# Other transfer costs in a planner, one column of weights ahead of the values, and VectorE subtracting the maximum of two tiles

## The chip, the cores and the metric

The kernel runs on one core of a Trainium2 chip. TensorE (PE) multiplies matrices, VectorE (DVE), ScalarE (ACT) and GpSimd (POOL) work on elements, and SyncE (SP) issues the transfers between the chip's memory (HBM) and the on-chip buffer (SBUF); TensorE writes its results to PSUM, which VectorE and ScalarE read. Each engine runs its instructions in the order in which they are written, and waits at an instruction until all that it needs is there. The metric is the device time of one execution in microseconds (us).

## The reference

Attention over 2 batches of 8 heads, 768 tokens, 64 numbers a head; each token sees the tokens less than 16 away, and 24 summaries, one for each block of 32 tokens (the maximum of the keys, the mean of the values). Two layers of a multilayer network follow, over 1536 tokens of 512 numbers with 2048 inner ones:

```python
k_sum = k.reshape(B, H, nb, block, D).max(axis=3)
v_sum = v.reshape(B, H, nb, block, D).mean(axis=3)
scores_l = scale * np.matmul(q, k.transpose(0, 1, 3, 2))       # masked to |i - j| < 16
scores_s = scale * np.einsum('bhsd,bhnd->bhsn', q, k_sum) + np.log(block)
a = softmax(concatenate([scores_l_m, scores_s]))
attn = a @ concatenate([v, v_sum])
...
h = x @ w_in;  g = np.maximum(h, 0.0) + np.log1p(np.exp(-np.abs(h)));  y = g @ w_out
h = np.maximum(y @ w_in2, 0.0);  out = h * h @ w_out2
```

## The kernel before, in words

**Attention.** The 1536 tokens are 12 tiles of 128. For a tile, TensorE multiplies transposed queries `qT` with `kaug` (24 key summaries and a window of 96 keys for each half of the tile, copied from the transposed keys `kT`) into the PSUM tile `sc` (tile 1 into `accp`). The softmax gives `s`, which TensorE transposes into `at`, and `at` times `vwin` (the window of values, and the 24 block means of values in its first partitions) gives the tile's output, kept as a high part `xh` and a residual `xl`. The block means are one product of TensorE from the whole values of a batch (`late`), copied to `vsum` and from there into `vwin`.

**Two ways through the softmax.** The letter of `STYLE` says which one a tile takes. In `m` (tiles 0 and 1) TensorE adds the mask itself, VectorE takes the negated maximum of a half tile (`mx`), and ScalarE takes the exponential of each of the 4 heads of a half with that maximum as its bias, 16 instructions for two tiles; VectorE then sums (`sm`) and takes reciprocals, and GpSimd multiplies. In `p` (tiles 2 to 11) VectorE adds the mask, GpSimd or VectorE subtracts the maximum, and one exponential does the whole tile.

**The network.** Its first layer's first four columns of weights (step `A`, lines 664 and 701: `h` and `accp`) run between the attention tiles, over 256 tokens at a time; all else runs after the attention, over 512 tokens. All weights and operands are split into a high and a low part and each product is three. A column of weights comes by two transfers of 512 KB into `raw`; its parts are made by `three` (ScalarE or VectorE), two joins on VectorE (line 614), a scaling, a high part (`wih`, `woh`) and a residual (`wil`, `wol`, GpSimd or VectorE).

**The order of the work.** `Plan` is a list scheduler that runs when the kernel is built. Each `op` has engines with an assumed duration, a due time, its inputs and outputs, and for a transfer its size `kb`. `run` moves a modelled time forward; on each engine it takes the ready operation with the earliest due time, chooses between two engines the one that would be done first (VectorE with 1.5 us to its disadvantage), and writes the instructions out in that order. A transfer is modelled as one queue: ready 1.6 us after its issue, `kb`/245 us long, usable 0.3 us later. Where TensorE would idle for more than 0.9 us in the model, `warm` writes filler products on `ident` (line 857). What is written is a fixed order, with the waits that the data need; the modelled times are not in it. `EARLY` is the number of weight columns whose transfers are due ahead of the first batch's values.

Of the kernel before, what the change touches and what calls it, by code (L numbers as in the profile page):

```python
# [13 lines left out]
ALU = mybir.AluOpType  # L14
# [17 lines left out]
KLAG = 6.0  # L32
EARLY = 2
LD_K = (8.0, 0.0)
# [4 lines left out]
DL = 32.0  # L39
PEB = 40.0  # L40
NS_T = 2
STYLE = "mmpppppppppp"

# [10 lines left out]
class Plan:  # L54
# [38 lines left out]
    def run(self, warm, banks, pool):  # L93
# [41 lines left out]
        while any(cand.values()):  # L135
# [27 lines left out]
            if kb:  # L163
                dma = max(dma, end + 1.6) + kb / 245.0
                end = dma + 0.3
            done[i] = end
# [19 lines left out]
def kernel(  # L186
# [192 lines left out]
    def ld_pair(src, u, place, due):  # L379
        b, i = divmod(u, NU)  # L380
        for z in range(2):
            op("SP", 0.6, due, lambda z=z: nc.sync.dma_start(  # L382
                out=PZ(place)[:, z].rearrange("p a (r d) -> p a r d", r=2),
                in_=src[b, 4 * z:4 * z + 4, 256 * i:256 * i + 256, :].rearrange("h (p r) d -> p h r d", r=2)),
                w=[(place, z)], kb=180)

# [42 lines left out]
    def ld_vb(b, due):  # L429
        op("SP", 0.8, due, lambda: nc.sync.dma_start(  # L430
            out=PL["V"], in_=v[b].rearrange("h (p r) d -> p h r d", r=VR)), w=["V"], kb=1017)

# [15 lines left out]
    def vsum_put(x, due):  # L448
        op("POOL", 1.3, due, lambda: nc.gpsimd.tensor_scalar(
            out=vwin[x][0:NS].rearrange("p j h d -> p j (h d)"),  # L450
            in0=vsum.rearrange("p (o x) -> p o x", o=1).to_broadcast([NS, 2, H * D]),
            scalar1=1.0, scalar2=1.0, op0=ALU.mult, op1=ALU.mult), r=["vsum", "z"], w=[("vsw", x)])

    def mk_kaug(t, due):
        i = t % NTB
        for j in range(2):
            c0 = 128 * i + 64 * j
            us = sorted({min(max((c0 + d - 16) // 128, 0), NTB - 1) for d in (0, 95)})
            op("POOL", 0.55, due, lambda j=j, c0=c0: nc.gpsimd.tensor_scalar(
                out=kaug[t % 2][:, :, j, NS:], in0=kT[:, :, c0:c0 + WIN],  # L460
                scalar1=1.0, scalar2=1.0, op0=ALU.mult, op1=ALU.mult),
                r=["z"] + [("kT", u, z) for u in us for z in range(2)], w=[("kw", t % 2, j)])

    def tile_sc(t, due):
# [4 lines left out]
        style = STYLE[t]  # L469
        pe_mask = style in "mn"  # L470

# [32 lines left out]
        for h0, h1 in halves:  # L504
# [14 lines left out]
            if pe_mask:  # L519
# [3 lines left out]
                def exps(hh=hh, sv=sv, mv=mv, rv=rv):  # L523
                    for p in range(NP):
                        nc.scalar.activation(out=sv[:, p], in_=scv(hh)[:, p], func=AF.Exp, bias=mv[:, p:p + 1],
                                             **({"accum_out": rv[:, p:p + 1]} if style == "n" else {}))
                op("ACT", NP * (0.55 if style == "n" else 0.37), due, exps, r=[(sck, hh), *mk],
                   w=sk + (rk if style == "n" else []), tab="exp")
            else:
# [362 lines left out]
```

## Time and profile before

| what | value |
|---|---|
| time, median of 3 (lowest to highest) | 620.82 us (620.57 to 621.85) |
| the profiled execution: its time, its span | 620.8 us, 619.0 us |
| busy in the span: TensorE, VectorE, ScalarE, GpSimd | 602.5, 312.1, 288.2, 202.0 us |
| TensorE's mean granted clock | 0.991 of full |
| chain that ended last, share of TensorE | 84% |
| moved by transfers | 51.34 MB |

Busy time is a sum over the whole span, and only TensorE is near it. The stages differ: attention and step A end near 110 us. In a timeline a row has its start, its duration and, in brackets, the idle time of its engine before it and what ended that. In tables of groups stand the count, the busy time and mean ns of one, and the idle time. L12 is line 12 of the kernel.

### The profile page before, as it was taken

How to read it: one execution, taken by the hardware profiler on the slowest of the kernel's cores; microseconds unless marked ns; L12 is line 12 of the kernel's file. 1: busy time of each engine (PE TensorE's matmuls, PEld its weight loads, DVE VectorE, ACT ScalarE, POOL GpSimd, SP SyncE). 2: the span in 40 equal slices, each digit the busy share in tenths (PEclk: the TensorE clock that was granted, in tenths of full speed). 3: DMA queues.
4: the chain of work that ended last, by engine and by line, in shares of the span. 5: the costliest groups of instructions: out<-in, count | busy, mean ns of one | idle time of the engine just before them, and what ended most of it. 6: DMA issues, size and time to landing. Idle time of an engine off the chain costs nothing.

```text
span 619.0 us, 9449 instructions
## 1 busy us (share of the span) xinstructions
PE 602.5 (97%) x3809; PEld 507.5 (82%) x3809; DVE 312.1 (50%) x449; ACT 288.2 (47%) x501; POOL 202.0 (33%) x197
## 2 busy tenths in 40 slices
PE   9798999999999999999999999999999999999996
PEld 7687988999788888888888888888888888888885
DVE  5788999726664133542146652247542533232332
ACT  4686888856653124542247643346412432221220
POOL 5877696535550042331138440116000410000000
PEclk9798999999999999999999999999999999999999
DMA  9999632423541014340024330114100100010011
GB/s 283 243 281 217 162 74 55 116 69 116 166 128 35 0 35 136 103 136 1 0 64 122 120 103 0 35 61 131 47 1 0 69 0 2 0 58 11 20 50 68
DMA packets 64524, 51.34 MB, mean 83 GB/s; under 512 B 36320, under 2 KB 58848, under 8 KB 64480
## 3 DMA queue, kind: packets, MB, share of 16 engines
q1 hardware_dynamic: 64480, 50.73, 28.6%
q8 instruction: 30, 0.49, 0.3%
q14 instruction: 14, 0.11, 0.1%
HBM read 47.58 MB, written 3.15 MB: 82 GB/s over the span
## 4 chain that ended last, share of the span: by engine, by line
PE 84%; DVE 8%; DMA 4%; ACT 2%; SPq 1%; issue 1%; POOL 0%; DVEq 0%; POOLq 0%
PE h L664 40%; PE accp L701 21%; PE acc L701 18%; DMA late<-in_v_dram 2%; DMA vwin<-in_v_dram 2%; DVE raw L614 2%; DVE mx L530 1%; DVE s L499 1%; PE ab L439 1%; PE ab L561 1%; DVE sm L516 1%; SPq L382 1%; PE ab L547 1%; DVE xl L571 0%; DVE sm L517 0%
## 5 line engine op out<-in xcount | busy, mean ns | idle before, releaser
L664 PE MATMUL h<-xh,wih 128*128 128x512 f32 (+1 forms) x432 | 159.9, 370 | 0.0
L664 PE MATMUL h<-xh,wil 128*128 128x512 f32 (+1 forms) x432 | 158.7, 367 | 0.0
L664 PE MATMUL h<-xl,wih 128*128 128x512 f32 (+1 forms) x432 | 158.7, 367 | 0.0
L614 DVE SCALAR_TENSOR_TENSOR raw<-raw 128x512 uint32<-128x512 uint32 x128 | 113.3, 902 | 52.8 <-ACT raw L609 39.8
L664 PEld LDWEIGHTS h<-xh,wih 128*128 128x128 f32 x432 | 81.5, 189 | 14.6 <-issue 0.6
L664 PEld LDWEIGHTS h<-xh,wil 128*128 128x128 f32 x432 | 81.3, 188 | 13.9
L664 PEld LDWEIGHTS h<-xl,wih 128*128 128x128 f32 x432 | 81.4, 188 | 13.7
L673 ACT ACTIVATE e<-h 128x512 f32<-128x512 f32 x48 | 28.8, 599 | 125.4 <-PE h L664 125.4
L675 DVE SCALAR_TENSOR_TENSOR h<-h,e 128x512 f32<-128x512 f32 x48 | 33.5, 698 | 103.2 <-ACT e L673 103.1
L671 ACT ACTIVATE h<-h 128x512 f32<-128x512 f32 (+1 forms) x60 | 29.8, 499 | 83.2 <-PE h L664 83.1
L308 POOL TENSOR_SCALAR wih<-raw 128x512 fp32r<-128x512 f32 x18 | 12.6, 703 | 150.5 <-PE h L664 142.1
L623 POOL TENSOR_TENSOR wol<-raw,woh 128x512 fp32r<-128x512 f32 x30 | 42.6, 1421 | 48.9 <-ACT woh L306 48.3
L623 POOL TENSOR_TENSOR wil<-raw,wih 128x512 fp32r<-128x512 f32 x31 | 42.6, 1374 | 28.9 <-ACT wih L306 27.4
L609 ACT ACTIVATE raw<-raw 128x512 uint32<-128x512 uint16 x59 | 39.3, 670 | 13.2 <-DMA raw<-in_moe_w_out_dram 7.5
L680 DVE TENSOR_TENSOR g1l<-h,g1h 128x512 fp32r<-128x512 f32 (+1 forms) x40 | 24.2, 606 | 31.9 <-ACT g1h L678 31.8
L723 DVE TENSOR_TENSOR part<-accp,part 128x512 f32<-128x512 f32 x24 | 16.0, 686 | 43.5 <-PE accp L701 43.5
L680 DVE TENSOR_TENSOR g2l<-h,g2h 128x512 fp32r<-128x512 f32 x28 | 19.3, 690 | 33.7 <-ACT g2h L678 33.5
L306 ACT ACTIVATE raw<-raw 128x512 f32<-128x512 f32 x41 | 27.5, 673 | 18.7 <-DVE raw L614 18.7
L680 DVE TENSOR_TENSOR g0l<-h,g0h 128x512 fp32r<-128x512 f32 (+1 forms) x40 | 24.1, 605 | 21.1 <-ACT g0h L678 20.9
L678 ACT ACTIVATE g0h<-h 128x512 fp32r<-128x512 f32 (+1 forms) x40 | 21.2, 534 | 16.4 <-DVE h L675 16.0
L536 POOL TENSOR_TENSOR s<-s,sm 128x960 f32<-128x960 f32 (+1 forms) x14 | 22.1, 1580 | 13.9 <-DVE sm L518 13.0
L678 ACT ACTIVATE g1h<-h 128x512 fp32r<-128x512 f32 (+1 forms) x40 | 21.4, 534 | 9.2 <-DVE h L675 8.9
(172 smaller groups left out, 1175.4 us busy)
## 6 DMA issues: line engine op xcount, KB each, us to landing
raw<-in_moe_w_in_dram SPq DMA_DIRECT2D x32, 512.0 KB, 4.2
raw<-in_moe_w_out_dram SPq DMA_DIRECT2D x32, 512.0 KB, 3.4
vwin<-in_v_dram SPq DMA_DIRECT2D x20, 192.0 KB, 5.7
part<-in_k_dram SPq DMA_DIRECT2D x12, 256.0 KB, 4.9
late<-in_v_dram SPq DMA_DIRECT2D x2, 1536.0 KB, 11.3
out_dram<-part SPq DMA_DIRECT2D x12, 256.0 KB, 2.1
part<-in_q_dram SPq DMA_DIRECT2D x10, 256.0 KB, 5.1
vwin<-in_v_dram SPq DMA_DIRECT2D x4, 160.0 KB, 5.2
```

Of the source, the lines that this page charges most:

```text
L306: nc.scalar.activation(out=out_, in_=in_, func=AF.Copy, **({} if mul is None else {"scale": mul}))
L536: op(("POOL", "DVE"), (1.8 * n + 0.1, 1.75 * n), due, lambda e, sv=sv, rv=rv, spread=spread: tt(e).tensor_tensor(out=sv, in0=sv, in1=sprea ...
L609: nc.scalar.activation(out=lo, in_=q4[:, :, 1], func=AF.Copy, scale=2.0 ** -13, bias=-4095.5 / 8192.0)
L614: nc.vector.scalar_tensor_tensor(out=lo, in0=hi, scalar=n, in1=lo, op0=how, op1=ALU.bitwise_or)
L623: op(("POOL", "DVE"), (1.4, 1.0), dv, lambda e: tt(e).tensor_tensor(out=ws[s][kl], in0=lo.bitcast(F32), in1=ws[s][kh].bitcast(F32), op=ALU ...
L664: nc.tensor.matmul(out=hview(st), lhsT=ws[s][wn][:, w_], rhs=xx[bl][:, kk, o:o + n], start=(kk == 0 and xx is xh and wn == "ih"), stop=(kk ...
L671: op("ACT", ta, due, lambda: nc.scalar.activation(out=hview(st), in_=hview(st), func=AF.Softplus), w=[H_], tab="sp")
L673: op("ACT", ta, due, lambda: nc.scalar.activation(out=e_t[st["g"] % 2], in_=hview(st), func=AF.Relu), r=[H_], w=[("e", st["g"] % 2)])
L675: op("DVE", tv, due, lambda: nc.vector.scalar_tensor_tensor(out=hview(st), in0=hview(st), scalar=0.0, in1=e_t[st["g"] % 2], op0=ALU.max, o ...
L678: op("ACT", ta, due, lambda: nc.scalar.activation(out=gview(st)[0], in_=hview(st), func=AF.Copy), r=[H_] + need, w=gk[0])
L680: op("DVE", tv, due, lambda: nc.vector.tensor_tensor(out=gview(st)[1], in0=hview(st), in1=gview(st)[0].bitcast(F32), op=ALU.subtract), r=[ ...
L701: nc.tensor.matmul(out=o, lhsT=a[:, sl], rhs=b, start=(st["first"] and c == 0 and not (A and m % 2)), stop=(st["last"] and c == 2 and not ...
```

## The change

The planner's transfer model is changed: a transfer is ready 1.2 us after its issue and usable 1.5 us after its end (1.6 and 0.3 before), and the sizes that stand for paired keys and queries and for the whole values are larger. One column of weights instead of two is due ahead of the values. The window copies `kaug` may go to VectorE as well, and the copies of block means `vsum_put` to ScalarE. Tiles 0 and 1 take the new way `d`: the mask is still added by TensorE, VectorE adds the negated maximum from PSUM into `s`, and one exponential does a half tile.

```diff
-EARLY = 2
+EARLY = 1
+KAUG_E = ("POOL", "DVE")
-STYLE = "mmpppppppppp"
+STYLE = "ddpppppppppp"
...
-                dma = max(dma, end + 1.6) + kb / 245.0
-                end = dma + 0.3
+                dma = max(dma, end + 1.2) + kb / 245.0
+                end = dma + 1.5
...   (ld_pair)
-                w=[(place, z)], kb=180)
+                w=[(place, z)], kb=206)
...   (ld_vb)
-            out=PL["V"], in_=v[b].rearrange("h (p r) d -> p h r d", r=VR)), w=["V"], kb=1017)
+            out=PL["V"], in_=v[b].rearrange("h (p r) d -> p h r d", r=VR)), w=["V"], kb=1090)
...
-        op("POOL", 1.3, due, lambda: nc.gpsimd.tensor_scalar(
-            out=vwin[x][0:NS].rearrange("p j h d -> p j (h d)"),
-            in0=vsum.rearrange("p (o x) -> p o x", o=1).to_broadcast([NS, 2, H * D]),
-            scalar1=1.0, scalar2=1.0, op0=ALU.mult, op1=ALU.mult), r=["vsum", "z"], w=[("vsw", x)])
+        op(("POOL", "ACT"), (1.15, 1.0), due, lambda e: copy(
+            e, vwin[x][0:NS].rearrange("p j h d -> p j (h d)"),
+            vsum.rearrange("p (o x) -> p o x", o=1).to_broadcast([NS, 2, H * D])), r=["vsum", "z"], w=[("vsw", x)])
...
-            op("POOL", 0.55, due, lambda j=j, c0=c0: nc.gpsimd.tensor_scalar(
-                out=kaug[t % 2][:, :, j, NS:], in0=kT[:, :, c0:c0 + WIN],
-                scalar1=1.0, scalar2=1.0, op0=ALU.mult, op1=ALU.mult),
+            op(KAUG_E, (0.55, 0.45)[:len(KAUG_E)], due, lambda e="POOL", j=j, c0=c0: copy(
+                e, kaug[t % 2][:, :, j, NS:], kT[:, :, c0:c0 + WIN]),
...
-        pe_mask = style in "mn"
+        pe_mask = style in "mnd"
...
+                if style == "d":
+                    op("DVE", 1.3 * n, due, lambda hh=hh, sv=sv, mv=mv, spread=spread: nc.vector.tensor_tensor(
+                        out=sv, in0=scv(hh), in1=spread(mv), op=ALU.add),
+                        r=[(sck, hh), *mk], w=sk)
+                    op("ACT", 0.2 + 0.8 * n, due, lambda sv=sv: nc.scalar.activation(out=sv, in_=sv, func=AF.Exp), w=sk, tab="exp")
+                else:
+                    op("ACT", NP * (0.55 if style == "n" else 0.37), due, exps, r=[(sck, hh), *mk],
+                       w=sk + (rk if style == "n" else []), tab="exp")
```

The new orders differ nearly everywhere in the attention phase. On TensorE the fillers ahead of the first transposes of keys are 15 (11 before), ahead of the first scores 6 (9), between the scores and the block means none (13), from there to tile 0's transposes 18 (9), then 6 (4), and later 6 and 7 (7 once). Three places follow; a name has its buffer number (`raw_75` to `raw_78` are the four places for incoming weights, `s_132` and `s_133` the even and the odd tiles).

SyncE's queue from the first weights on, before:

```order
L599 DMA raw_75<-in_moe_w_in_dram 128x4x256
L602 DMA raw_76<-in_moe_w_out_dram 128x1024
L599 DMA raw_77<-in_moe_w_in_dram 128x4x256
L602 DMA raw_78<-in_moe_w_out_dram 128x1024
L430 DMA late<-in_v_dram 128x8x384
L425 DMA vwin_130<-in_v_dram 80x8x64
L425 DMA vwin_130<-in_v_dram 96x8x64
L425 DMA vwin_131<-in_v_dram 96x8x64 x2
L350 DMA late<-in_q_dram 128x8x64 x2
```

and now:

```order
L604 DMA raw_75<-in_moe_w_in_dram 128x4x256
L607 DMA raw_76<-in_moe_w_out_dram 128x1024
L431 DMA late<-in_v_dram 128x8x384
L426 DMA vwin_130<-in_v_dram 80x8x64
L426 DMA vwin_130<-in_v_dram 96x8x64
L604 DMA raw_77<-in_moe_w_in_dram 128x4x256
L426 DMA vwin_131<-in_v_dram 96x8x64 x2
L607 DMA raw_78<-in_moe_w_out_dram 128x1024
L351 DMA late<-in_q_dram 128x8x64 x2
```

The second column's two transfers moved behind the values and behind the windows of tiles 0 and 1.

ScalarE from the exponentials of tile 0 on (`at_134` is tile 0's transposed weights), before:

```order
L525 ACTIVATE s_132<-sc,mx_136 128x120 x8
L525 ACTIVATE s_133<-accp,mx_137 128x120 x4
L444 ACTIVATE vsum<-ab_141 24x128 x4
L525 ACTIVATE s_133<-accp,mx_137 128x120 x4
L306 ACTIVATE at_134<-ab_142 120x512
L306 ACTIVATE at_134<-h_108 120x512
L306 ACTIVATE wih_87<-raw_77 128x512
```

and now:

```order
L530 ACTIVATE s_132<-s_132 128x480 x2
L445 ACTIVATE vsum<-ab_141 24x128 x4
L307 ACTIVATE vwin_130<-vsum 24x1024
L307 ACTIVATE vwin_131<-vsum 24x1024
L307 ACTIVATE at_134<-ab_142 120x512
L530 ACTIVATE s_133<-s_133 128x480
L307 ACTIVATE at_134<-h_108 120x512
L614 ACTIVATE raw_77<-raw_77 128x512
L530 ACTIVATE s_133<-s_133 128x480
L614 ACTIVATE raw_78<-raw_78 128x512
```

Tile 1's exponentials stood ahead of tile 0's transposed weights and now stand behind the first of them; two `three` steps stand there too.

VectorE at the total of tile 3 (`sm_139`), before:

```order
L680 TENSOR_TENSOR g0l<-h_109,g0h 128x256
L614 SCALAR_TENSOR_TENSOR raw_75<-raw_75 128x512
L611 TENSOR_SCALAR raw_76<-raw_76 128x512
L611 TENSOR_SCALAR raw_77<-raw_77 128x512
L516 TENSOR_REDUCE sm_139<-s_133 128x8
L517 TENSOR_SCALAR sm_139<-sm_139 128x8
```

and now:

```order
L619 SCALAR_TENSOR_TENSOR raw_75<-raw_75 128x512
L370 TENSOR_REDUCE ks<-ab_142 128x4x4
L370 TENSOR_REDUCE ks<-ab_141 128x4x4
L515 TENSOR_REDUCE sm_139<-s_133 128x8
L516 TENSOR_SCALAR sm_139<-sm_139 128x8
L517 RECIPROCAL sm_139<-sm_139 128x8
L619 SCALAR_TENSOR_TENSOR raw_75<-raw_75 128x512
L619 SCALAR_TENSOR_TENSOR raw_76<-raw_76 128x512
```

The two `three` steps ahead of the total are gone from VectorE.

## Rows read from the trace of the kernel before

**Rows 1.** Windows: stretch, its length, busy us per engine, clock, DMA share, GB/s.
```profile
0.00:36.27 36.27, 31.52 (x463) 26.48 (x463) 25.38 (x44) 22.09 (x47) 24.38 (x47) 0.91 1.00 254
36.27:60.00 23.73, 20.17 (x258) 17.48 (x259) 19.35 (x30) 17.53 (x31) 17.55 (x17) 0.93 1.03 262
60.00:110.00 50.00, 47.08 (x661) 43.54 (x662) 49.62 (x69) 42.37 (x68) 38.45 (x32) 1.00 0.46 108
110.00:619.00 509.00, 503.72 (x2438) 419.99 (x2436) 217.73 (x310) 206.26 (x357) 121.65 (x104) 1.00 0.19 60
```

**Rows 2.** Waits of TensorE, 36.27 to 110 us: total us, times, longest.
```profile
PE ab L561 <- DMA vwin<-in_v_dram: 2.4, 2, 1.8
PE sc L491 <- DVE s L499: 1.1, 2, 0.6
...
PE ab L547 <- DVE xl L571: 0.5, 1, 0.5
```

**Rows 3.** Timeline of TensorE from the end of the scores to step A.
```profile
17.07 1.59 PE L857 MATMUL ab<-ident 128*128 128x256 bf16 x13
22.00 2.78 PE L439 MATMUL ab<-late,sel 128*24 128x128 f32 x48 [3.33 <-DMA late<-in_v_dram]
24.70 2.10 PE L857 MATMUL h<-ident 128*128 128x256 bf16 x9
26.60 1.06 PE L547 MATMUL ab<-ident,s 128*120 128x128 f32 x4
...
36.27 0.36 PE L664 MATMUL h<-xh,wih 128*128 128x256 f32 x1
```

**Rows 4.** Chain that ended last: start, us, what.
```profile
9.20 12.75 DMA late<-in_v_dram
```

**Rows 5.** Windows of the trace, transfers and clock early.
```profile
12.00:18.00 6.00, 6.00 (x108) 4.65 (x105) 4.70 (x9) 4.34 (x7) 3.59 (x5) 1.00 1.04 375
21.00:27.00 6.00, 5.00 (x59) 3.81 (x60) 4.73 (x12) 2.75 (x11) 4.31 (x5) 0.50 0.92 185
52.00:55.00 3.00, 3.00 (x53) 2.25 (x50) 3.00 (x4) 1.88 (x4) 2.36 (x3) 0.50 0.85 150
```

**Rows 6.** Timeline of ScalarE, 16 to 35 us.
```profile
16.75 0.70 ACT L609 ACTIVATE raw<-raw 128x512 uint32<-128x512 uint16 x1 [0.64 <-DMA raw<-in_moe_w_out_dram]
...
18.50 2.12 ACT L525 ACTIVATE s<-sc,mx 128x120 f32<-128x120 f32 x8 [0.49 <-DVE mx L520]
...
34.39 0.60 ACT L306 ACTIVATE xh<-h 128x512 fp32r<-128x512 f32 x1 [0.47 <-PE h L561]
```

**Rows 7.** Timeline of VectorE, 46 to 50 us.
```profile
46.62 0.43 DVE L611 TENSOR_SCALAR raw<-raw 128x512 uint32<-128x512 uint32 x1 [1.03 <-DMA raw<-in_moe_w_out_dram]
49.01 0.43 DVE L611 TENSOR_SCALAR raw<-raw 128x512 uint32<-128x512 uint32 x1 [1.97 <-DMA raw<-in_moe_w_in_dram]
49.36 1.15 DVE L516 TENSOR_REDUCE sm<-s 128x8 f32<-128x960 f32 x1
```

**Rows 8.** Timeline of TensorE, the second block means.
```profile
52.05 2.78 PE L439 MATMUL ab<-late,sel 128*24 128x128 f32 x48
```

**Rows 9.** VectorE's groups to 110 us, then line 614 to 120 us (ns min/median/max).
```profile
L614 DVE SCALAR_TENSOR_TENSOR raw<-raw 128x512 uint32<-128x512 uint32 x26 | 25.8, 1013 | 1.3 <-ACT raw L609 1.2
L499 DVE TENSOR_TENSOR s<-sc,mask 128x480 f32<-128x480 f32 x18 | 11.1, 642 | 0.7 <-PE sc L491 0.7
...
L623 DVE TENSOR_TENSOR wol<-raw,woh 128x512 fp32r<-128x512 f32 x2 | 4.1, 2048 | 0.1
...
L611 DVE TENSOR_SCALAR raw<-raw 128x512 uint32<-128x512 uint32 x4 | 2.6, 660 | 3.0 <-DMA raw<-in_moe_w_in_dram 2.0 <-DMA raw<-in_moe_w_out_dram 1.0
...
L614 DVE SCALAR_TENSOR_TENSOR raw<-raw x28: 642/832/2283, 13.0 to 116.3; 128x512 uint32<-128x512 uint32 x28
```

**Rows 10.** GpSimd's groups to 110 us, then line 459 over the span.
```profile
L532 POOL TENSOR_TENSOR s<-s,mx 128x960 f32<-128x960 f32 x9 | 16.9, 1877 | 5.8 <-DVE mx L530 5.7
...
L459 POOL TENSOR_SCALAR kaug<-kT x24: 504/516/963, 8.3 to 96.7; 128x384 f32<-128x384 f32 x24
```

More of the change, by code (lines that the diff above doesn't have):

```diff
@@ L526, in exps @@
                                              **({"accum_out": rv[:, p:p + 1]} if style == "n" else {}))
-                op("ACT", NP * (0.55 if style == "n" else 0.37), due, exps, r=[(sck, hh), *mk],
-                   w=sk + (rk if style == "n" else []), tab="exp")
+                if style == "d":
[6 more added lines that the diff above has]
+                       w=sk + (rk if style == "n" else []), tab="exp")
             else:
```

## The prediction

> **What bounds the kernel now.** I read four windows of the trace first [rows 1]. From 110 us to the end TensorE is busy for 503.72 of 509 us, so whatever the attention phase does, this stretch follows behind it unchanged: the kernel's time is moved only by when the products of the multilayer part stop waiting, that is, by what TensorE loses before 110 us. It loses 4.75 us idle before 36.27 us (where the first product of the feed-forward part starts), 3.56 us from there to 60 us, and 2.92 us from 60 to 110 us. In the last of these VectorE is busy 49.62 of 50 us, and until 60 us the DMA engines are full (share 1.00 and 1.03). So there are two suppliers to look at: transfers early, VectorE later.
>
> The waits of TensorE after the first product [rows 2] name them: 2.4 us for the window of values `vwin`, 1.1 us for VectorE's mask addition, 0.5 us for its residual `xl`. Then the timeline of the start [rows 3]: both score blocks are done at 17.1 us, filler products run to 18.66, TensorE sits 3.33 us until the whole values `late` have landed at 22.00, forms their block means (2.78 us), runs nine fillers and transposes tile 0's weights only at 26.60. The values were issued at 9.20 and took 12.75 us [rows 4], behind four weight transfers. The clock fell to half after that idle time: 0.50 in 21 to 27 us, and again in 52 to 55 us [rows 5], so the second block-mean product also takes 2.78 us [rows 8].
>
> **The change, part by part.** The profiled execution took 620.8 us, 619.0 of it the span and 1.8 around it; the median shown is 620.82, so both count as one.
>
> *The start.* The second pair of weight transfers (2 x 512 KB) now stands behind the values. The transfers moved 375 GB/s in 12 to 18 us [rows 5], so 1.05 MB is 2.8 us, and the values should land at 21.95 - 2.8 = 19.1 us. TensorE has longer fillers ahead of the key transposes (15 for 11) and shorter ones ahead of the scores (6 for 9); what this moves ends before 19.1 and is covered by the wait for the values. The block means run at once, 19.1 to 21.9, and then 18 fillers stand before tile 0's transposes. A filler took 2.10/9 = 0.233 us at half clock and 1.59/13 = 0.122 at full [rows 3], so 2.2 to 4.2 us: the transposes start at 24.1 to 26.1 us, against 26.60.
>
> What follows gets longer. The two tiles' 16 exponentials were 0.27 us each (8 in 2.12 [rows 6]), 4.2 us; four of half a tile at 0.60 (as a 512-wide ScalarE copy [rows 6]) make 2.4. But VectorE's four subtractions (0.64 each by the mask addition [rows 9], 2.6 us) come ahead of them, and on ScalarE tile 1's two exponentials and two weight preparations now stand between the copies of tile 0's transposed weights and the `xh` of tile 1. In that stretch ScalarE has 16 instructions instead of 12, and only 0.47 us of waiting right ahead of that `xh` to hide them in; four times 0.60 to 0.70 [rows 6] is 2.4 to 2.8, and the lower end less 0.47 is about 2.0. So the first product comes 9.67 + 2.0 = 11.7 us after the transposes: 35.8 to 37.8 us, middle 36.8 against 36.27, **+0.5** (from -0.5 to +1.5). The subtractions lie in a stretch where VectorE is busy only 25.38 of 36.27 us [rows 1], and hide there. The delayed second weights are wanted only for the second product, 3.4 us after the first; if they were late by more than that, the excess would come on top.
>
> *The waits for transfers, 40 to 52 us.* With the new transfer costs, the window of tile 2 (the one that TensorE waits for) is issued one and two weight transfers sooner: 1.4 us for 512 KB at 375 GB/s. And on VectorE the total of tile 3 (`sm`, 49.36) no longer stands behind two weight preparations that waited 1.03 and 1.97 us for their transfers [rows 7]; these two go to ScalarE. Of TensorE's 2.4 us [rows 2] about two thirds go, **-1.5** (bounds 0 and -2.4). With less idle time before the second block-mean product the clock may stay up; at full clock that product can take no less than half of 2.78, so from 0 to -1.4: **-0.7**. Two new runs of fillers (6 and 7 for the one of 7) add 6 x 0.122 = **+0.7**.
>
> *VectorE from 36 us on.* Counted in the two orders up to the last `xl`: it loses four `three` steps (0.66 each) and two residuals `wol` (2.05 each), 6.7 us, and the 3.0 us of waits above; it gains one whole-tile subtraction (two mask additions' worth, 1.28), three `kaug` copies (0.50 to 0.52 on GpSimd [rows 10], 0.5 taken) and one transposed-weight copy (0.64): 3.4 us [rows 9]. Net 6.3 us less on an engine without slack. TensorE can give back only what it loses to VectorE there, 1.1 + 0.5 us of waits [rows 2] out of 2.92 idle: I take **-1.2** (bounds 0 and -2.9). ScalarE gets six preparations more and four high-part copies less; it is busy 42.37 of 50 us [rows 1], which covers it; without that cover it would cost 2 x 0.70.
>
> The sum: +0.5 - 1.5 - 0.7 + 0.7 - 1.2 = -2.2, and 620.8 - 2.2 = **618.6 us**. From 110 us on the weights come in nearly the same order and TensorE has no gap to give.
>
> **A rule against it.** The joins of two halves of a weight on VectorE read two operands from SBUF; they took 0.642 us at best, 2.283 at worst and 1.013 in the mean while GpSimd was at work, and a small preparation 0.43 alone and 0.660 in the mean [rows 7, 9]. GpSimd's own `kaug` copies run from 504 to 963 ns [rows 10]. The Trainium skill, GPSIMD Engine Reference, Specifications, says that its SBUF interfaces are shared with VectorE and contended by VectorE instructions in a two-port mode or with two SBUF inputs; this trace agrees, by the spread 0.642 to 2.283. By it the moved subtraction and copies would cost more than their bare durations. That is a rival with a price of its own, below.
>
> **The rivals.**
> 1. *The start slips (slower).* If the values land no earlier, because what is issued right behind them shares the engines (12.75 us for 1.5 MB is three times what 375 GB/s needs), then block means at 21.95, 18 fillers at half clock to 28.9, first product at 40.6: +4.3 instead of +0.5. With the other terms -2.7 this is 622.4. It turns slower than before when the first product comes later than 36.27 + 2.7 = 39.0 us, i.e. the values after 20.3 us with cold fillers. For it: the long landing and 18 fillers which TensorE must run whether or not tile 0 is ready. Against: 1.05 MB less ahead. Chance 0.18.
> 2. *Nothing comes through.* The moved operations run beside GpSimd as the joins do: the subtraction at 1.28 x 2.283/0.642 = 4.6 us instead of 1.28, each copy at 0.96 instead of 0.5: +4.7 of the 6.3 us saved on VectorE. Then the VectorE term is 0, and half of the wait for the windows (0.75) is passed on as well: 618.6 + 1.2 + 0.75 = 620.5. Chance 0.20. For it: VectorE has no slack. Against: GpSimd itself gets fewer whole-tile operations (a subtraction at 1.88 and three copies less [rows 10]).
> 3. *Both suppliers give all.* The clock stays up from the start (first product at 35.8, -0.5), the window waits go (-2.4), the second product runs at full clock (-1.4), all VectorE waits go (-1.6), fillers +0.7: -5.2, 615.6. Chance 0.17.
>
> **How the numbers follow.** 0.45 for the forecast, between 616.9 and 619.5, 0.18, 0.20 and 0.17 for the rivals. This kernel's measurement can tell 0.2%, 1.24 us, from no change: faster below 619.6, slower above 622.0. Forecast and rival 3 are faster, 0.62; rival 2 is the same, 0.20; rival 1 slower, 0.18. The range for 8 in 10 leaves out the outer half of rivals 1 and 3: 615.6 to 622.4.
>
> **What would show it.** Right: the block means start near 19 us, tile 0's transposes at 24 to 26, the first product at 36 to 38; no wait of TensorE for `vwin` over 1 us near 50; VectorE not waiting for transfers between 45 and 50; TensorE without a gap from about 107 us. The clock in the second block-mean product tells whether the 0.7 was earned. Wrong: a first product after 39 us; joins and subtractions over 2 us in 60 to 110 us; or a new wait after 110 us for a weight's low part, since the weights' work is shared out anew between GpSimd and ScalarE there.

## The result, and the profile after

The changed kernel takes 624.23 us (median of eight executions), the kernel before 620.67 beside it: a ratio of 1.0052, interval 1.0035 to 1.0068. One of the eight took 1204.71 us and is left out of the ratio; the other seven took 622.26 to 625.71. The change makes the kernel slower by some 3.3 us. The profiled execution is the slowest of the seven, 625.71, with a span of 624.0, so what its trace shows adds up to more than that. The windows of its trace (length, busy us of TensorE, its weight loads, VectorE, ScalarE, GpSimd, then clock, DMA share, GB/s) answer to [rows 1] and [rows 5]:

```profile
0.00:36.27 36.27, 29.66 (x424) 23.95 (x425) 22.75 (x43) 21.50 (x37) 20.41 (x42) 0.91 0.96 238
36.27:60.00 23.73, 18.95 (x201) 16.60 (x199) 19.49 (x29) 16.11 (x27) 16.11 (x14) 0.86 1.03 251
60.00:110.00 50.00, 46.60 (x665) 42.52 (x665) 45.65 (x66) 40.87 (x69) 38.02 (x33) 1.00 0.50 122
110.00:624.00 514.00, 509.26 (x2531) 425.32 (x2529) 224.28 (x317) 208.85 (x359) 129.55 (x110) 1.00 0.19 60
...
54.00:60.00 6.00, 5.30 (x29) 4.81 (x25) 4.79 (x7) 4.61 (x9) 2.69 (x3) 0.50 1.01 225
```

TensorE idles 6.61, 4.78 and 3.40 us in the first three, 4.75, 3.56 and 2.92 before: +1.86, +1.22, +0.48; behind 110 us it is 0.54 less. TensorE's busy time is 1.97 us more over the span (604.46 for 602.49). With the 3.02 us of idle time that makes the 5.0 by which the two spans differ. An estimate of what the 1.97 holds: the clock of 0.86 for 0.93 in the second window takes (0.14 - 0.07) x 23.73 = 1.7 us, and 58 fillers for 53 at 0.12 us another 0.6. TensorE's start (start, duration, idle time before and what ended it), for [rows 3, 8]:

```profile
20.90 2.77 PE L440 MATMUL ab<-late,sel 128*24 128x128 f32 x48 [4.06 <-DMA late<-in_v_dram]
23.61 3.41 PE L862 MATMUL h<-ident 128*128 128x256 bf16 x18
26.86 0.60 PE L552 MATMUL ab<-ident,s 128*120 128x128 f32 x4
...
37.95 0.36 PE L669 MATMUL h<-xh,wih 128*128 128x256 f32 x1
...
52.18 0.66 PE L362 MATMUL ab<-ident,part 128*128 128x128 f32 x4 [3.23 <-ACT at L307]
...
54.82 1.12 PE L362 MATMUL ab<-ident,part 128*128 128x128 f32 x4 [0.70 <-ACT qT L307]
...
63.04 1.51 PE L440 MATMUL ab<-late,sel 128*24 128x128 f32 x48
```

The values, issued 0.9 us sooner [rows 4],

```profile
8.30 12.56 DMA late<-in_v_dram
```

landed 1.1 us sooner [rows 3], tile 0's transposes came no sooner, and the first product 1.7 us later. TensorE's waits from 36.27 to 110 us (total us, times, longest) answer to [rows 2]:

```profile
PE ab L362 <- ACT at L307: 3.2, 1, 3.2
PE h L669 <- DVE g0l L685: 2.2, 3, 1.1
...
PE h L669 <- DVE g1l L685: 0.8, 1, 0.8
```

In place of the wait for `vwin` stands one for ScalarE's `at`: its copies empty the PSUM tile `ab`, which TensorE wants for its next transposes. ScalarE's timeline shows why they are late:

```profile
46.48 1.01 ACT L539 ACTIVATE s<-s 128x960 f32<-128x960 f32 x1
50.99 0.67 ACT L614 ACTIVATE raw<-raw 128x512 uint32<-128x512 uint16 x1 [3.49 <-DMA raw<-in_moe_w_out_dram]
51.56 1.07 ACT L307 ACTIVATE at<-ab 120x512 f32<-120x512 f32 x2
53.60 0.68 ACT L614 ACTIVATE raw<-raw 128x512 uint32<-128x512 uint16 x1 [0.97 <-DMA raw<-in_moe_w_in_dram]
```

The two `three` steps that left VectorE [rows 7] wait on ScalarE for the same weights, with tile 2's `at` copies behind the first and `qT` behind the second. Nor did tile 2's window come sooner. Its second half, the last row but one of SyncE's here, was issued at 41.95 us; the row of transfers under it says that it landed 10.1 us later, at 52.1. In the kernel before TensorE had it at 50.94, as the row under that shows:

```profile
38.43 1.05 SPq L426 DMA_DIRECT2D vwin<-in_v_dram  x1
39.59 2.27 SPq L607 DMA_DIRECT2D raw<-in_moe_w_out_dram  x1
41.95 0.49 SPq L426 DMA_DIRECT2D vwin<-in_v_dram  x1
42.52 3.08 SPq L604 DMA_DIRECT2D raw<-in_moe_w_in_dram  x1
```

```profile
vwin<-in_v_dram SPq DMA_DIRECT2D x1, 192.0 KB, 10.1
```

```profile
50.94 1.18 PE L561 MATMUL ab<-at,vwin 120*64 120x64 f32 x28 [0.54 <-DMA vwin<-in_v_dram]
```

After TensorE's idle time the clock is at half (0.50 in 54 to 60 us). From 60 us on TensorE waits for VectorE's `g0l` and `g1l`:

```profile
71.56 0.39 PE L669 MATMUL h<-xh,wih 128*128 128x256 f32 x1 [0.84 <-DVE g1l L685]
...
82.95 0.39 PE L669 MATMUL h<-xh,wih 128*128 128x256 f32 x1 [1.07 <-DVE g0l L685]
...
104.45 0.39 PE L669 MATMUL h<-xh,wih 128*128 128x256 f32 x1 [0.49 <-DVE g0l L685]
```

VectorE's timeline has what moved to it (lines 537 and 309) and what TensorE waited for; under it the view of the copies' line (ns min/median/max, first and last start):

```profile
43.59 2.53 DVE L537 TENSOR_TENSOR s<-s,mx 128x960 f32<-128x960 f32 x1
...
81.17 1.20 DVE L516 TENSOR_SCALAR sm<-sm 128x8 f32<-128x8 f32 x1
...
82.52 0.37 DVE L685 TENSOR_TENSOR g0l<-h,g0h 128x256 fp32r<-128x256 f32 x1
82.81 1.98 DVE L309 TENSOR_SCALAR kaug<-kT 128x384 f32<-128x384 f32 x1
...
101.85 2.21 DVE L309 TENSOR_SCALAR kaug<-kT 128x384 f32<-128x384 f32 x2
103.99 0.41 DVE L685 TENSOR_TENSOR g0l<-h,g0h 128x256 fp32r<-128x256 f32 x1
```

```profile
L309 DVE TENSOR_SCALAR kaug<-kT x3: 351/1948/1980, 82.8 to 102.1; 128x384 f32<-128x384 f32 x3
```

and GpSimd beside these:

```profile
80.56 1.78 POOL L537 TENSOR_TENSOR s<-s,mx 128x960 f32<-128x960 f32 x1
...
82.79 1.78 POOL L541 TENSOR_TENSOR s<-s,sm 128x960 f32<-128x960 f32 x1
...
101.88 1.97 POOL L537 TENSOR_TENSOR s<-s,mx 128x960 f32<-128x960 f32 x1
```

A copy of 0.35 us takes 1.95 to 1.98 while GpSimd multiplies or subtracts a whole tile, and both slow ones end 0.22 us behind that instruction. The one of 0.35 started 0.03 us ahead of it. On GpSimd a copy took 0.5 [rows 10]. The copies explain only the last of TensorE's waits above, 0.49 us: the `g0l` of 82.52 ran ahead of the copy. What it stood behind is a small scaling of sums, 1.20 us beside GpSimd's subtraction and 0.17 at 49.34, where GpSimd was idle. The kernel before has such scalings too. VectorE's group of joins, on the other hand, fell from 1013 ns in the mean to 811 [rows 9]:

```profile
L619 DVE SCALAR_TENSOR_TENSOR raw<-raw 128x512 uint32<-128x512 uint32 x27 | 21.6, 811 | 5.0 <-ACT raw L614 4.4 <-ACT raw L307 0.6
```

### The profile page after: what moved, and what is told of

Same layout as the page of the kernel before. It is cut to its first block, busy times and chain, and to the rows that moved or that the text cites. A ratio compares the mean times of both kernels' runs of the same rounds, so it can differ in the third digit from the quotient of the medians.

```text
span 624.0 us, 9466 instructions
## 1 busy us (share of the span) xinstructions
PE 604.5 (97%) x3814; PEld 508.4 (81%) x3814; DVE 312.2 (50%) x452; ACT 287.3 (46%) x489; POOL 204.1 (33%) x198
## 4 chain that ended last, share of the span: by engine, by line
PE 85%; DVE 5%; DMA 4%; POOL 2%; ACT 2%; SPq 1%; issue 1%; DVEq 0%; POOLq 0%
PE h L669 40%; PE accp L706 22%; PE acc L706 18%; DMA late<-in_v_dram 2%; DMA raw<-in_moe_w_in_dram 2%; PE ab L552 1%; DVE raw L619 1%; PE ab L566 1%; SPq L383 1%; DVE sm L515 1%; PE h L862 1%; POOL kaug L309 1%; POOL s L537 1%; DVE sm L516 1%; DVE mx L535 0%
## 5 line engine op out<-in xcount | busy, mean ns | idle before, releaser
L619 DVE SCALAR_TENSOR_TENSOR raw<-raw 128x512 uint32<-128x512 uint32 x128 | 111.1, 887 | 36.5 <-ACT raw L614 20.7
L309 POOL TENSOR_SCALAR wih<-raw 128x512 fp32r<-128x512 f32 x22 | 17.4, 790 | 161.7 <-PE h L669 150.1
L628 POOL TENSOR_TENSOR wol<-raw,woh 128x512 fp32r<-128x512 f32 x32 | 45.0, 1408 | 33.0 <-ACT woh L307 32.0
L614 ACT ACTIVATE raw<-raw 128x512 uint32<-128x512 uint16 x63 | 41.8, 673 | 8.8 <-DMA raw<-in_moe_w_out_dram 7.0
L307 ACT ACTIVATE raw<-raw 128x512 f32<-128x512 f32 x44 | 29.6, 674 | 20.7 <-DVE raw L619 20.6
L541 POOL TENSOR_TENSOR s<-s,sm 128x960 f32<-128x960 f32 (+1 forms) x14 | 22.8, 1628 | 13.0 <-DVE sm L517 12.6
```

The lines of the kernel that those rows point to most:

```text
L307: nc.scalar.activation(out=out_, in_=in_, func=AF.Copy, **({} if mul is None else {"scale": mul}))
L309: tt(e).tensor_scalar(out=out_, in0=in_, scalar1=1.0 if mul is None else mul, scalar2=1.0, op0=ALU.mult, op1=ALU.mult)
L614: nc.scalar.activation(out=lo, in_=q4[:, :, 1], func=AF.Copy, scale=2.0 ** -13, bias=-4095.5 / 8192.0)
L619: nc.vector.scalar_tensor_tensor(out=lo, in0=hi, scalar=n, in1=lo, op0=how, op1=ALU.bitwise_or)
L628: op(("POOL", "DVE"), (1.4, 1.0), dv, lambda e: tt(e).tensor_tensor(out=ws[s][kl], in0=lo.bitcast(F32), in1=ws[s][kh].bitcast(F32), op=ALU ...
```

## The experiments

Four questions came one after the other. T1: the step that waits on ScalarE holds up what is behind it. T2: the transfers are late, whatever stands on ScalarE. (The expectations call them the second column's. What is awaited near 50 us are the third column's `w_out` and the fourth's `w_in`, issued at 39.59 and 42.52; the second column's `three` steps began at 28.96 and 30.02.) T3: the start is longer (a: by the fillers; b: by ScalarE's copies of the block means; c: by tile 1's exponentials behind them). W or R: the parts' own work costs the time, or the new order that the planner writes. In the table idle is the window's length less TensorE's busy time in the profiled execution, from the same views as above; each ratio is to executions of the kernel before beside that kernel (medians 620.34 to 620.93).

| kernel | median us | ratio to before, interval | idle to 36.27, to 60, to 110 us | clock 36 to 60 | fillers |
|---|---|---|---|---|---|
| before | 620.67 | 1 | 4.75, 3.56, 2.92 | 0.93 | 53 |
| changed | 624.23 | 1.0052 (1.0035 to 1.0068) | 6.61, 4.78, 3.40 | 0.86 | 58 |
| s1 | 623.09 | 1.0044 (1.0027 to 1.0061) | 5.63, 3.71, 3.58 | 0.86 | 58 |
| s2 | 623.27 | 1.0043 (1.0027 to 1.0059) | 8.57, 3.19, 3.65 | 1.00 | 58 |
| s3 | 624.17 | 1.0055 (1.0040 to 1.0070) | 6.77, 3.39, 3.58 | 0.86 | 40 |
| s5 | 623.91 | 1.0047 (1.0032 to 1.0063) | 6.33, 4.53, 3.80 | 1.00 | 58 |
| s6 | 623.47 | 1.0049 (1.0033 to 1.0064) | 8.12, 5.02, 3.96 | 1.00 | 40 |
| s7 | 623.66 | 1.0040 (1.0025 to 1.0056) | 6.84, 4.01, 3.29 | 0.86 | 58 |
| s8 | 624.50 | 1.0062 (1.0048 to 1.0076) | 8.77, 3.22, 3.35 | 0.93 | 40 |
| p1 | 623.75 | 1.0047 (1.0028 to 1.0066) | 6.63, 4.83, 4.98 | 0.93 | 51 |
| b1 | 624.81 | 1.0065 (1.0047 to 1.0083) | 8.16, 2.89, 4.90 | 1.00 | 51 |
| b2 | 624.41 | 1.0059 (1.0042 to 1.0075) | 5.59, 2.09, 4.67 | 1.00 | 93 |
| b3 | 626.94 | 1.0103 (1.0082 to 1.0124) | 7.27, 3.91, 3.49 | 0.86 | 90 |
| b4 | 625.93 | 1.0090 (1.0073 to 1.0108) | 5.65, 5.20, 5.90 | 0.93 | 71 |
| r1 | 622.11 | 1.0019 (1.0007 to 1.0031) | 6.05, 5.40, 3.73 | 1.00 | 45 |
| r2 | 629.48 | 1.0126 (1.0103 to 1.0150) | 7.20, 3.52, 5.86 | 0.93 | 62 |
| c1 | 620.79 | 0.9993 (0.9980 to 1.0006) | 6.65, 2.57, 2.48 | 0.93 | 53 |
| c2 | 627.68 | 1.0107 (1.0088 to 1.0126) | 13.87, 1.69, 3.51 | 0.94 | 53 |
| c4 | 622.09 | 1.0020 (1.0007 to 1.0032) | 7.05, 4.48, 2.48 | 0.95 | 53 |
| c5 | 629.45 | 1.0131 (1.0110 to 1.0152) | 14.04, 1.37, 3.41 | 0.83 | 53 |

### The changed kernel's order, edited by hand

**s1.** On ScalarE the `three` steps go behind what they held up:

```diff
-three raw_76; at_134 x2; three raw_77; qT; xh
+at_134 x2; three raw_76; qT; xh; three raw_77
```

> Only ScalarE's order at tile 2 is changed: the two three steps on the second column's weights stand behind tile 2's transposed weights and behind xh of tile 2, where they wait for their transfers without holding anything else up. T1 (the step waiting for its transfer holds up the copies behind it): TensorE's idle time of 3.23 us at 49 us falls under 1 us, the product of tile 2 starts at about 50.5 instead of 52.77, the clock stays up, and the kernel takes 620.5 to 621.5 us, 0.5% less than the changed kernel. T2 (all transfers of the second column are late, whatever stands on ScalarE): the product of tile 2 then waits for the second half of its window, which landed at 52.1, the idle time is renamed to a wait for a transfer, and the time stays at 623 to 624.5.

The wait for `at` is gone, and TensorE's timeline has another just behind it:

```profile
49.89 1.76 PE L591 MATMUL ab<-at,vwin 120*64 120x64 f32 x28 [2.27 <-DMA vwin<-in_v_dram]
```

T1 named the wait rightly and its worth wrongly: the second half of the window was late too, as T2 has it. The intervals of s1 and of the changed kernel overlap nearly wholly.

**s2.** SyncE's order as before:

```diff
-V, vwin 0 x2, w_in 2, vwin 1 x2, w_out 2
+w_in 2, w_out 2, V, vwin 0 x2, vwin 1 x2
```

> Only SyncE's order is changed: the second column's two weight transfers stand ahead of the values again, as in the kernel before; every other engine keeps the changed kernel's order. T1: the values land near 22 us, the first product comes 1 us later (39), the step on ScalarE finds its weights sooner, so that the idle time near 50 us shrinks to about 1 us: 622 to 623. T2: queries, keys and weights land 2 to 3 us sooner, the idle time near 50 and the half clock after it go, the start loses about 1 us: 620.5 to 622. A third way (the start decides: everything runs behind the first product): 625 to 626.

TensorE waits for no transfer between 36 and 60 us, and the clock there is 1.00. T1 had forecast a short wait there too, and 622 to 623, so this run does not tell the two apart. But the values land at 22.99, for which TensorE stands 6.06 us,

```profile
22.99 2.77 PE L465 MATMUL ab<-late,sel 128*24 128x128 f32 x48 [6.06 <-DMA late<-in_v_dram]
```

and the first product comes at 39.56. What T2 said of the middle holds, and its time (620.5 to 622) does not: the start pays for it.

**s3.** The 18 fillers out:

```diff
-filler x18; transposes of tile 0
+transposes of tile 0
```

> The 18 fillers between the block means and tile 0's transposes are left out, nothing else is changed (they compute nothing that is used). T3a (the fillers that TensorE must run hold tile 0 up): the transposes start at 23.7 instead of 26.86 and the first product at 35 instead of 37.95; if all of it lasts, 621 us. T3b (ScalarE's copies of the block means, 23.74 to 26.88, stand ahead of the copies of tile 0's weights): the product of tile 0 starts under 1 us sooner, the first product near 37.3, and the time stays at 623.5 to 624.5. T2 adds that even an earlier first product is given back near 50 us, where the transfers decide.

T3b's time holds. The transposes ran at 22.52, right behind the block means (19.82), and TensorE then waited for ScalarE, where the copies into `vwin` stood ahead of those into `at`:

```profile
26.48 0.43 PE L590 MATMUL h<-at,vwin 120*64 120x64 f32 x2 [1.84 <-ACT at L331]
27.45 1.97 PE L590 MATMUL h<-at,vwin 120*64 120x64 f32 x30 [0.55 <-ACT at L331]
```

The first product came at 37.83, 18.0 us behind the block means and not 17.05, so leaving the fillers out gave nothing. Part of this is the clock, which neither theory named: 0.57 from 26 to 34 us, against 0.98 in the changed kernel, where the 30 products took 1.15 us and not 1.97.

**s5.** Tile 1's exponentials ahead on ScalarE:

```diff
-vsum x4; vwin x2; at; exp; at; three; exp
+exp; exp; vsum x4; vwin x2; at; at; three
```

> ScalarE alone is changed, at the start: tile 1's two exponentials stand ahead of the copies of the block means (VectorE had subtracted at 21.77 and 23.50, and ScalarE idled to 23.74 while they stood behind tile 0's transposed weights). Theory T3c (tile 1's exponentials behind the copies make the start longer): the product of tile 1 comes 4.1 us behind tile 0's as in the kernel before, not 5.8 to 6.7, and the kernel takes 622 to 622.5. Rival (TensorE is busy there anyway, the order of its own work decides): only the wait of 0.42 us for GpSimd's s goes, 623.5 to 624.

The product of tile 1 came 6.7 us behind tile 0's, not 4.1: T3c falls. TensorE was busy for 6.52 of these 6.68 us, at a clock of 0.74: its own order and the clock decide there.

**s6.** Fillers out, exponentials ahead, and the copies on GpSimd again. They ended up behind tile 0's product in program order, so that this kernel, and s8, leave the block means out of tile 0's product:

```diff
-filler x18
-ScalarE: vsum x4; vwin x2; at; exp
+ScalarE: exp; exp; vsum x4; at
+GpSimd: wol; vwin; vwin
```

> The start alone: the 18 fillers out, tile 1's exponentials ahead of the copies of the block means, and the two copies of the block means into the windows on GpSimd again. T3 (ScalarE's queue is what lies between the values and the first product): the product of tile 0 starts 5.5 to 6 us after the block means' start (6.7 without the fillers alone, 7.6 to 8.2 with them) and the first product 14 to 14.5 us after it as in the kernel before, instead of 16.5 to 17: about 621.5. T2 (the transfers near 50 us decide): an earlier first product only makes TensorE wait longer for the window of tile 2 and its weights, 623 to 624.

Tile 0's product started 5.9 us behind the block means, as expected, but the first product 18.0 behind them, because TensorE now waited 1.83 us for queries and 0.73 for `s`; and 3.46 us for `at` near 50 us. The clock was 0.79 from 26 to 34 us. A shorter queue ahead of tile 0 gave nothing by the first product.

**s7.** s1, and the second half of tile 2's window ahead of `w_out` on SyncE:

```diff
-vwin 2; w_out; vwin 2; w_in
+vwin 2; vwin 2; w_out; w_in
```

> The middle alone: the two three steps behind tile 2's transposed weights, as in the first experiment, and on SyncE the second half of tile 2's window issued ahead of the w_out weights, which SyncE holds up until GpSimd has freed their place (2.0 us of its queue). If the wait of TensorE near 49 us is the sum of these two queues, the wait of 2.27 us for the window goes under 0.5 us and the clock stays up: 621 to 622. If the transfers themselves are the limit, w_out lands later instead, and the time stays at 623 to 623.5 with a new wait for a weight before 60 us.

The waits for the window fell from 2.27 to 1.11 us (0.51 and 0.60), and a wait for a weight came behind them: ScalarE stood 2.92 us for `w_out`, ahead of `qT`, and TensorE 1.47 us for that `qT`. This is the second of the two forecasts. The DMA engines are full from 36 to 60 us (share 1.02), and the order only chooses which transfer is late.

**s8.** s6 and s7 together. 

> The start of the one and the middle of the other together. If the two losses are separate queues, their gains add up: 619 to 620.5, at or under the kernel before. If the transfers bound both, what the start gives is waited for in the middle: 621.5 to 623.

The gains did not add: 624.50 us, above both forecasts, with the first product at 39.64 and 2.21 us for `xl` at 55.79 as the new wait.

### One part at a time, planned anew

**p1.** `EARLY` back to 2 in the changed kernel:

```diff
-EARLY = 1
+EARLY = 2
```

> One number of the change undone: two columns of weights ahead of the values again; the new transfer costs, engines and way d stay, and the planner writes a new order. T2 (the second column behind the values is the cause): 620 to 621.5, near the kernel before, with no idle time over 1.5 us near 50 us. Rival (what moved to ScalarE and VectorE is the cause, not the transfers): 623 to 625, with a three step on ScalarE or a subtraction on VectorE still ahead of TensorE's longest wait.

T2's forecast of 620 to 621.5 fails, the rival's time holds. TensorE idles more than before in all three windows, by 1.88, 1.27 and 2.06 us; its longest wait behind the first product is 3.12 us for VectorE's `ks` at 45.61. **b1 to b4** put one part alone into the kernel before: way d, transfer costs, one column, engines.

```diff
-STYLE = "mmpppppppppp"
+STYLE = "ddpppppppppp"       (b1)
-end + 1.6, dma + 0.3, kb 180 and 1017
+end + 1.2, dma + 1.5, kb 206 and 1090       (b2)
-EARLY = 2
+EARLY = 1       (b3)
-kaug: POOL; vsum_put: POOL
+kaug: POOL, DVE; vsum_put: POOL, ACT       (b4)
```

> One part alone on the kernel before: tiles 0 and 1 take way d; transfer costs, engines and the two columns ahead of the values stay. The planner writes 51 fillers (53 before, 58 changed). Theory W (what is lost comes from the transfers' new order and the work moved to ScalarE): 620 to 621, as before, or a little less, since 12 exponentials go. Theory R (every new plan draws new orders near 50 us and from 60 to 110 us, which the planner's model can't tell apart, whatever the part): 622 to 624, with another wait than the ones seen.

> One part alone on the kernel before: the new transfer costs in the planner. It writes 93 fillers (53 before): it now thinks that data comes later and fills the idle time that it sees. If those 40 fillers stand where TensorE would have been ready, they cost up to 40 x 0.12 = 4.8 us: 624 to 625.5. If they lie in waits that are there anyway: 621 to 622.

> One part alone on the kernel before: one column of weights ahead of the values. 90 fillers (53 before). T2 (the second column late is the cause near 50 us): values near 20, first product near 36, but a wait for a window or a weight of 2 to 4 us between 45 and 55 us: 622.5 to 625. If an earlier landing of the values is worth more than the late column: under 620.

> One part alone on the kernel before: window copies may go to VectorE and copies of the block means to ScalarE. 71 fillers (53 before). Theory W: ScalarE's queue between the values and the first product is longer by a copy, first product near 37, 621.5 to 622.5. Theory R: 622 to 624 with a loss that comes later than 40 us. If GpSimd was what held TensorE up: under 620.

Each part alone is as slow as all together or slower, by 0.59 to 1.03%; these add up to 3.2%, and the whole change costs 0.52%. b1, b3 and b4 took longer than any theory had forecast. The costs of parts do not add, and they do not lie in one place. TensorE's longest wait behind the first product is in b1 1.81 us at 72.60 for `g1l`, in b2, which has 40 more fillers, 1.71 at 67.56 for `g1l`, in b3 2.79 at 50.20 for `at`, behind a `three` step, as in the changed kernel, and in b4 3.19 at 54.44 for VectorE's mask addition. Up to 36.27 us b1 and b3 idle more than before too, by 3.41 and 2.52 us.

**r1, r2.** The planner's assumed 0.12 us from an operation's end to its user becomes 0.13 or 0.11; all work stays:

```diff
-    SEM = 0.12
+    SEM = 0.13       (r1; r2: 0.11)
```

> The kernel before with one assumed number of the planner changed from 0.12 to 0.13 us (the time from an operation's end to its user's start); operations, engines allowed, ways and transfers are all those of before. The planner writes another order (45 fillers instead of 53). Theory R (the loss is that of a new order): 622 to 625, with TensorE's losses in other places than before. Theory W (the changed parts' own work costs it): 620 to 621, as before; the 8 fillers fewer are worth up to 1.0 us.

> The same with 0.11 instead of 0.12 us (62 fillers). Theory R: 622 to 626. Theory W: 620 to 621.7, the upper end if all nine more fillers count at 0.12 us.

Ten nanoseconds of a model's number cost 0.19% and 1.26%. r2's worst wait on TensorE, the instruction of VectorE that it comes from, and GpSimd's rows beside that:

```profile
91.58 0.58 PE L664 MATMUL h<-xl,wih 128*128 128x256 f32 x1 [3.44 <-DVE xl L571]
```

```profile
83.93 5.53 DVE L614 SCALAR_TENSOR_TENSOR raw<-raw 128x512 uint32<-128x512 uint32 x1
```

```profile
83.98 1.30 POOL L623 TENSOR_TENSOR wil<-raw,wih 128x512 fp32r<-128x512 f32 x1
85.25 0.65 POOL L308 TENSOR_SCALAR woh<-raw 128x512 fp32r<-128x512 f32 x1
85.87 1.78 POOL L532 TENSOR_TENSOR s<-s,mx 128x960 f32<-128x960 f32 x1
87.62 1.29 POOL L623 TENSOR_TENSOR wol<-raw,woh 128x512 fp32r<-128x512 f32 x1
```

A join of 0.64 us [rows 9] lasted 5.53, to 89.46, beside GpSimd instructions that followed each other to 88.91.

### The content in the order of the kernel before

**c1.** Way d, nothing planned anew:

```diff
-ScalarE: exp 128x120 x4
+VectorE: s = sc + mx;  ScalarE: exp 128x480
```

> Way d for tiles 0 and 1 in the order of the kernel before, nothing planned anew: where four exponentials of a half tile stood, VectorE subtracts and ScalarE takes one exponential. Theory R: the part itself costs or gives little, 620 to 621, against 624.81 when it was planned anew. Theory W: the subtractions on VectorE (4 x 0.64 us ahead of the totals) make the first product later by 1 to 2.5 us: 621.5 to 623.

0.9993 (0.9980 to 1.0006): the part costs nothing, where planned anew it cost 0.65%. In its profile the values landed at 23.35 and the first product came at 38.1, later than in the changed kernel; it still ends as the kernel before does. Its windows:

```profile
0.00:36.27 36.27, 29.62 (x423) 24.09 (x424) 26.29 (x46) 18.88 (x34) 24.29 (x46) 0.91 1.01 247
36.27:60.00 23.73, 21.16 (x275) 18.76 (x276) 20.84 (x30) 18.13 (x33) 17.58 (x17) 0.93 1.06 258
60.00:110.00 50.00, 47.52 (x683) 44.05 (x679) 48.86 (x69) 42.71 (x68) 38.93 (x33) 1.00 0.48 114
```

Of the 1.9 us lost by 36 us 1.4 come back by 110: the second window idles 2.57 us for 3.56, the third 2.48 for 2.92.

**c2, c5.** The second column's transfers behind the values, alone (c2), and with way d and the copies of the block means on ScalarE (c5). The order that SyncE got is neither the change's nor what the expectations say: `w_out` stands ahead of `w_in`, and both ahead of tile 1's window:

```diff
-w_in 2, w_out 2, V, vwin 0 x2, vwin 1 x2
+V, vwin 0 x2, w_out 2, w_in 2, vwin 1 x2
```

> The order of the kernel before, in which SyncE alone is changed: the second column's two weight transfers are issued behind the values and the windows of tiles 0 and 1. T2 (the transfers' order decides): the values land 1 to 3 us sooner, but the first product can't come much before 36 since tile 0's and tile 1's own work lies between, and the weights, queries and keys that follow come 1 to 3 us later: 622 to 624. Theory R (only new orders cost): 620 to 621, the sooner values giving what the later weights take.

> Nearly the whole content of the change in the order of the kernel before, nothing planned anew: way d for tiles 0 and 1, the copies of the block means on ScalarE, the second column's transfers behind the values (left out are the three window copies on VectorE and the planner's new transfer costs, which have no work of their own). Theory R: 620 to 621.5, not 624. If the content costs on its own: 622.5 to 625, as the changed kernel.

Both fell far outside what either theory gave. In c2 the values land at 20.07, but tile 0's weights come 10.21 us later than TensorE wants them, since ScalarE's kept order has the second column's `three` steps ahead of the exponentials (TensorE's row, then ScalarE's, then SyncE's):

```profile
32.88 1.11 PE L572 MATMUL ab<-ident,s 128*120 128x128 f32 x4 [10.21 <-POOL s L561]
```

```profile
25.89 1.22 ACT L634 ACTIVATE raw<-raw 128x512 uint32<-128x512 uint16 x2 [11.15 <-DMA raw<-in_moe_w_in_dram]
```

```profile
12.71 3.58 SPq L627 DMA_DIRECT2D raw<-in_moe_w_out_dram  x1
16.34 0.67 SPq L624 DMA_DIRECT2D raw<-in_moe_w_in_dram  x1
```

In c5 the same wait is 10.73 us. This is T1's mechanism by itself: where a transfer moves and the steps that use it stay, these hold up what is behind them. But part of the wait may be the exchange, since `w_in`, which ScalarE wants first, was issued 3.6 us behind `w_out`. So the two kernels price neither the change's order of transfers nor its whole content.

**c4.** The kernel before, with tile 2's window ahead of the `w_in` weights:

```diff
-w_out, w_in, vwin 2 x2
+w_out, vwin 2 x2, w_in
```

> The kernel before with the two transfers of tile 2's window issued ahead of the second column's first w_in transfer, all else in its order. If the window was only held up in SyncE's queue, TensorE's 2.4 us of waits for it fall to under 1 us and the kernel takes 618.8 to 619.6. If the transfers are full there, the window comes 0.5 us sooner and the weight later by as much: 620 to 621.

The waits for the window fell from 2.4 to 0.36 us; VectorE then stood 3.25 us for `w_in`, with `xl` behind that step, and TensorE 3.20 us for `xl`:

```profile
57.32 1.73 PE L573 MATMUL ab<-ident,s 128*120 128x128 f32 x8 [3.20 <-DVE xl L597]
```

At 622.09 us this kernel, too, is above both forecasts.

No kernel here beats the one before. In the third window the changed kernel and the seven with its order there idle 3.29 to 3.96 us, c1 and c4, with the old order, 2.48. But c2 and c5 have the old order there too, run 6 to 10 us late, and idle 3.51 and 3.41, so the window does not show that the order alone makes the difference.

## Why the prediction was wrong, step by step

- *The landing of the values (19.1).* 20.90 in the profiled execution, and 19.05, 19.82, 19.42, 19.29, 20.29 and 19.23 in s1, s3, s5, s6, s7 and s8, whose queue is the same up to there. Three more kernels with one column ahead have 20.30 (b3), 20.07 (c2) and 19.44 (c5). The ten with two columns ahead have 22.00 to 23.43, and the 22.00 from which I worked is the lowest. The means are 19.8 and 22.8, 3.0 us apart, so the 2.8 us for 1.05 MB was right.
- *From there to the first product (17.7 us).* 17.05, and 16.5 in s1; 14.27 before. So the +0.5 (-0.5 to +1.5) was near: +1.7 in the profile, -0.7 in s1 (35.53).
- *The waits for transfers, -1.5.* This is the step that failed. I let the window come sooner and the wait of the two weight steps vanish with their move to ScalarE. The wait moved with them, to a queue where tile 2's `at` copies stood behind: 3.23 us for 2.4. And a place further ahead in SyncE's queue was no earlier time: the second half of the window landed at 52.1, where TensorE had it at 50.94 in the kernel before. In s1, s7 and c4 the wait went from one of these transfers to another, and none of the three is faster than the kernel before.
- *The clock, -0.7.* It went the other way, an estimated (0.14 - 0.07) x 23.73 = +1.7, behind the longer idle time. The second block means did run at full clock (1.51 us), but products ahead of them had run at half (0.50 in 54 to 60 us).
- *Fillers, +0.7.* Five more, 0.6.
- *VectorE, -1.2.* Idle time in the third window rose by 0.48. VectorE was less busy (45.65 for 49.62) and later all the same where TensorE waited for it. I counted its busy time, where what comes ahead of `g0l` and `g1l` decides. The subtraction took 2.53 us, not 1.28, and the three copies 4.3 in all (351, 1948 and 1980 ns), not 1.5. Rival 2 named this mechanism, with 0.96 as the dearest copy. The Trainium skill, Trainium Architecture — The Big Picture, What this means for kernel authors, calls the port pair that VectorE and GpSimd share an exclusive lock and not a split of bandwidth; these rows agree, since the two slow copies last until 0.22 us behind GpSimd's instruction beside them. How much the copies cost the kernel is not shown: by the order of the rows they stand ahead of one wait of TensorE, 0.49 us at 104.45, and a kernel with them back on GpSimd and all else kept was not run.
- *The frame.* I added prices of parts as if the order around them stayed. r1, r2 and c1 show what that leaves out: an order drawn anew for no reason costs 0.2 to 1.3% here, 1.2 to 7.8 us, where no term of my sum was over 1.5. And an earlier or later first product is not a gain or loss by itself: s1 had it at 35.53 in its profile and takes 2.4 us more than the kernel before, c1 at 38.1 and takes the same.

Rival 1 gave the right sign, with a first product at 40.6 that did not come. That a new order costs time is shown by r1 and r2; which features of an order decide is not: nothing here predicts 622.11 for r1 and 629.48 for r2. All eight kernels that were planned anew are slower than the one before, and whether its order is a lucky one is not shown. Nor is it shown how the changed kernel's 0.52% divides between its order and its content: of the four parts only way d was priced with the order kept (c1), and c2 and c5 have another order of transfers than the change.

## What to carry to other kernels

Where a planner writes the order, price a change twice: with the order kept, and against plans drawn from numbers moved by nothing that matters; a difference inside that spread (here 0.2 to 1.3%, from two such plans) can't be told from the order's. A step that waits for a transfer keeps its wait when it moves to another engine: look at what stands behind it there. And where transfers are full, an edit that ends one wait picks the next.

## What the runs showed of the hardware

VectorE instructions on SBUF beside GpSimd instructions stretched far beyond their own length: a join of 0.64 us to 5.53 beside four in a row, a copy of 0.35 to 1.98, a scaling of 128x8 numbers from 0.17 to 1.20. In the changed kernel's third window four such scalings end 0.02 to 0.03 us behind the GpSimd instruction beside them. And the landing of the values, with the same transfers issued ahead of them, varied between 19.05 and 20.90 us in seven kernels' profiled executions, 1.85 us, where the change was meant to move it by 2.8: one profile before and one after do not measure such a shift.
